# The inverse transform's last stage: one 96 by 96 block-diagonal matmul, or two of 48 by 48 in the row halves of the array

## The chip, the cores and the metric

The kernel runs on one core of a Trainium2 chip. The metric is the device time of one execution in microseconds, the median of several runs. Five engines work side by side, each through its own list of instructions in order: TensorE (PE in the profile; its weight loads are listed as PEld), VectorE (DVE), ScalarE (ACT), GpSimd (POOL), and SyncE (SP), which here only issues DMAs. Matmul results land in PSUM, eight banks of 512 fp32 words per partition.

## The reference

Eight sequences of 3072 rows of 256 numbers go through a Fourier layer, and the result through a feed-forward layer with a three-way maximum:

```python
X = np.fft.rfft(x, axis=1)
Yr = Xr @ w_r - Xi @ w_i + b_r
Yi = Xr @ w_i + Xi @ w_r + b_i
Yr = np.sign(Yr) * np.maximum(np.abs(Yr) - lam, 0.0)      # lam = 0.01, the same for Yi
y = np.fft.irfft(Yr + 1j * Yi, n=3072, axis=1)
h = np.maximum(np.maximum(y @ w1, y @ w2), y @ w3)        # 256 -> 768
out = h @ w_out                                           # 768 -> 256
```

## The kernel before

The length 3072 is split as 48 x 64, and each transform is done in two matmul stages with tables that the host makes. A batch is one of the eight sequences. It goes through: `stage_a` (48-point transform; two row halves of the array, at partitions 0 to 47 and 64 to 111, and two column halves, fp32), a round trip through DRAM (`a_d`), `stage_b` (64-point transform, px), `stage_w` (the complex weights, py, then bias and soft threshold), `stage_q` (64-point inverse, pz), another round trip through DRAM (`z_d`), and then, chunk by chunk, the last 48-point inverse stage, `inverse` (pi). There are 8 chunks in a batch, 64 in all, each of 384 output positions.

After `inverse` a chunk goes through the feed-forward layer in six slots, one for each 128 of the 768 hidden columns: `up` (12 matmuls of 384 columns into two pu banks, then the maximum and a split), and one slot later `down` (pd, 9 matmuls of 256 columns, and over the last slots 18 more for the third weight, which is folded with w_out).

Nearly every operand is held as two fp16 parts, high and low, and a product is three matmuls: high x high, high x low, low x high (`mm3`, lines 133 to 135). So lines 133 to 135 appear under many tiles in the profile. The split itself is `split_scaled` (lines 127 and 128): an ACT copy that rounds to fp16, then a DVE subtraction for the rest.

The order of work: the main loop (lines 853 to 878) writes `up`, `down` and then what a list of events holds for that slot, which are the stages of the next batch. The event list (lines 689 to 703) is written out by hand with positions in slots. Around the change, `load_z` of the next chunk is called in slot 1, `split_z` in slot 3, `inverse` in slot 4. Its result is used from slot 0 of the next chunk, one `up` and one `down` later. The framework's scheduler then lays down each engine's list, with its own estimates of cost; on ACT, for instance, the copy of the next z stands between the two copies of pi in many chunks.

The tiles that matter here:

- zq, one buffer: a quad of z, 96 partitions (p, m) by 4 x 256 fp32, where p is one of two groups of four n2 positions and m one of 48 coefficients. Two DMAs on SP's queue fill it (line 713).
- zh and zl, one buffer each: its two fp16 parts (lines 720 to 723).
- ga_sb, the table: for each of 32 quads a 96 by 96 matrix with two 48 by 48 blocks on the diagonal and zeros elsewhere, in two fp16 parts (lines 49 to 53, 154).
- pi, taken by `ff_tile` from the ring of four PSUM banks called "ff", which px, py, pz and pa use as well. `inverse` takes one bank for each half h of the 256 columns, does 12 matmuls into it, and splits it into yh and yl; then comes the other h.
- xq, the input rows: its rows 32 to 63 are set to zero on POOL before the DMA (line 413). These are POOL's main work.

Of the kernel before, what the change touches and what calls it, by code (L numbers as in the profile page):

```python
# [9 lines left out]
F32 = mybir.dt.float32  # L10
F16 = mybir.dt.float16
# [9 lines left out]
T_SCALE, Y_SCALE, H_SCALE, Q_SCALE = 2.0**-15, 2.0**-14, 2.0**-23, 2.0**12  # L21


def dft_tables():

    n, n1n, n2n = 3072, 48, 64
    n1, n2, tp = np.arange(n1n), np.arange(n2n), 2 * np.pi
    fa, ga = np.zeros((n1n, n1n)), np.zeros((n1n, n2n, n1n))
    for m in range(46):
        k1, c = 1 + m // 2, m % 2
        ph = tp * ((k1 * n1) % n1n) / n1n  # L40
        fa[:, m] = np.cos(ph) if c == 0 else -np.sin(ph)
        ph = tp * ((k1 * (n2n * n1[None, :] + n2[:, None])) % n) / n
        ga[m] = (2.0 / n) * (np.cos(ph) if c == 0 else -np.sin(ph))
    alt = (-1.0) ** n1
    fa[:, 46], ga[46] = 1.0, 1.0 / n
    fa[:, 47], ga[47] = alt, alt[None, :] / n
    fa2 = np.zeros((112, 64))
    fa2[0:48, 0:48] = fa2[64:112, 0:48] = fa
    g5 = ga.reshape(n1n, 8, 2, 4, n1n)
    ga2 = np.zeros((2, n1n, 8, 4, 2, n1n))  # L50
    for p in range(2):
        ga2[p, :, :, :, p] = g5[:, :, p]
    ga2 = ga2.reshape(96, 32, 96)
    sg = np.where(n2 >= 32, -1.0, 1.0)

    def forward(k1):
        ang = tp * ((n2[:, None] * (k1 + n1n * n2[None, :])) % n) / n
        co, si = np.cos(ang), np.sin(ang)
        b = np.zeros((2, n2n, 2, n2n))
        b[0, :, 0], b[1, :, 0] = co, si  # L60
        b[0, :, 1], b[1, :, 1] = -si * sg, co * sg
        return b.reshape(128, 128)

    ang = tp * ((n2[:, None] * n2[None, :]) % n2n) / n2n
    co, si = np.cos(ang), np.sin(ang)
    q = np.zeros((2, n2n, 2, n2n))
    q[0, :, 0], q[1, :, 0] = co, -si * sg[:, None]
    q[0, :, 1], q[1, :, 1] = si, co * sg[:, None]
    bs, qs = np.zeros((2, n2n, 2, n2n)), np.zeros((2, n2n, 2, n2n))
    alt = (-1.0) ** n2  # L70
    bs[0, :, 0, 0], bs[0, :, 1, 0] = 1.0, alt
    qs[0, 0, 0, :], qs[1, 0, 0, :] = 1.0, alt
    for f in range(1, n2n):
        c, k = (0, n1n * f) if f < 32 else (1, 24 + n1n * (f - 32))
        ph = tp * ((k * n2) % n) / n
        bs[c, :, 0, f], bs[c, :, 1, f] = np.cos(ph), -np.sin(ph)
        qs[0, f, c, :], qs[1, f, c, :] = 2 * np.cos(ph), -2 * np.sin(ph)
    q, bs, qs = (v.reshape(128, 128) for v in (q, bs, qs))
    mb = [forward(k1) for k1 in range(1, 24)] + [bs]
    mq = [q, qs]  # L80

    def halves(v, scale):
        v = v * 2.0**scale
        hi = v.astype(np.float16)
        return np.ascontiguousarray(np.stack([hi, (v - hi).astype(np.float16)], 1))

    return (
        fa2.astype(np.float32),
        halves(ga2, SG),
        halves(np.stack(mb, 1), SB),  # L90
        np.ascontiguousarray(np.stack(mq + mb, 1)).astype(np.float32),
        np.eye(128, dtype=np.float32),
    )
# [3 lines left out]
def fourier_maxout_kernel(  # L97
    ctx: ExitStack, tc: tile.TileContext, x, w_r, w_i, b_r, b_i, w1, w2, w3, w_out, fa, ga, mb, mq, ident, out
):
    nc = tc.nc  # L100
    NB, S, D = x.shape
    FF = w1.shape[1]
    P = 128
    N1, N2 = 48, 64
    XR = 112
    KD = D // P
    NF = FF // P
    NQ = 4
    NCH = N2 // 8
    NT = 8 * N1  # L110
# [3 lines left out]
    const = ctx.enter_context(tc.tile_pool(name="const", bufs=1))  # L114
    fft = ctx.enter_context(tc.tile_pool(name="fft", bufs=2))
# [9 lines left out]
    def split_scaled(hi, lo, src, scale):  # L125
        h = hi if hi.dtype == F16 else hi.bitcast(F32)
        nc.scalar.activation(out=hi, in_=src, func=AF.Copy, scale=scale)  # L127
        nc.vector.scalar_tensor_tensor(  # L128
            out=lo, in0=src, scalar=scale, in1=h, op0=ALU.mult, op1=ALU.subtract
        )  # L130

    def mm3(o, lh, ll, rh, rl, start=True, stop=True, **kw):
        nc.tensor.matmul(o, lh, rh, start=start, stop=False, **kw)  # L133
        nc.tensor.matmul(o, lh, rl, start=False, stop=False, **kw)  # L134
        nc.tensor.matmul(o, ll, rh, start=False, stop=stop, **kw)  # L135
# [4 lines left out]
    def ff_tile(name):  # L140
        tag = spare[0]
        if len(spare) > 1:
            spare.append(spare.pop(0))
        return ps.tile([P, 512], F32, name=name, tag=tag, bufs=4 if tag == "ff" else 2)
# [6 lines left out]
    mb_all = const.tile([P, 4 * NJP * P], F16, name="mb_all")  # L151
    mb_sb = mb_all.rearrange("p (i k m) -> p i k m", i=2, k=2 * NJP)
    mb_f = mb_all.bitcast(F32).rearrange("p (k m) -> p k m", k=2 * NJP)
    ga_sb = const.tile([96, 2, N2 // 2, 2 * N1], F16, name="ga_sb")
    wch = const.tile([P, KD, 4, D], F16, name="wch")
    wcl = const.tile([P, KD, 4, D], F16, name="wcl")
    wuh = const.tile([P, 2, KD, FF], F16, name="wuh")
# [12 lines left out]
    def quad_tile(name):  # L170
        return fft.tile([XR, NQ * D], F32, name=name, bufs=1 if name == "zq" else 2)
# [213 lines left out]
    st = {}  # L385
# [303 lines left out]
    for q in range(NCH + 2, NB * NCH):  # L689
        b, i = divmod(q, NCH)  # L690
        p = i if b == 1 else (b - 2) * SLOTS + NF * i + 2
# [3 lines left out]
    for b in range(1, NB):  # L695
        for k in range(-2, NJP + 1):
            p = 8 + 2.2 * (k + 2) if b == 1 else (b - 1) * SLOTS + 2.8 * (k + 2)
# [10 lines left out]
            fn(i)  # L708

    def load_z(b, c):  # L710
        zq = quad_tile("zq")[0:96]
        for p in range(2):
            nc.sync.dma_start(
                out=zq[p * N1:p * N1 + N1].rearrange("p (n d) -> p n d", n=NQ),
                in_=batch(b, "z")[:, 8 * c + 4 * p:8 * c + 4 * p + 4, :],
            )
        st["zq"] = zq

    def split_z(b):
        zh = fft.tile([96, NQ, D], F16, name="zh", bufs=1)  # L720
        zl = fft.tile([96, NQ, D], F16, name="zl", bufs=1)
        split_scaled(*(t.rearrange("p n d -> p (n d)") for t in (zh, zl)), st["zq"], st[b, "su"][0][0:96])
        st["z"] = zh, zl

    def inverse(b, c):
        zh, zl = st["z"]
        yh, yl = (ffn.tile([P, KD, NT], F16, name=n, bufs=2) for n in ("yh", "yl"))
        for h in range(KD):
            py = ff_tile("pi")
            pv = py[:, 0:NT].rearrange("q (p i m) -> q i p m", p=2, i=NQ)  # L730
            for n2 in range(NQ):
                mm3(
                    pv[:, n2], *(t[:, n2, h * P:(h + 1) * P] for t in (zh, zl)),
                    *(ga_sb[:, i, c * NQ + n2, :].rearrange("q (p m) -> q p m", p=2) for i in range(2)),
                )
            split_scaled(
                *(t[:, h].rearrange("p (m n) -> p m n", n=8) for t in (yh, yl)),
                py[:, 0:NT].rearrange("p (n m) -> p m n", n=8), Y_SCALE,
            )
        return yh, yl  # L740

# [102 lines left out]
    for q in (NCH, NCH + 1):  # L844
        split_x(q)
        stage_a(q)
    load_z(0, 0)
    split_z(0)
    y = inverse(0, 0)
    del spare[1:]  # L850
    spare[0] = "ff"
# [61 lines left out]
```

## Time and profile before

| what | value |
|---|---|
| time, median of 3 runs | 1835.04 us (1834.65 to 1837.48) |
| profiled execution | 1835.95 us, span 1833.8 us, granted TensorE clock 0.987 |
| matmuls into pi (three lines of 512) | 1536, median 207 ns recorded each |
| splits of pi | 128 ACT copies of 490 ns, 128 DVE subtractions of 551 ns |
| splits of z | 64 ACT copies of 1148 ns, 64 DVE subtractions of 1276 ns |
| zero-fills on POOL (xq) | 56 of 942 ns |

A recorded matmul includes the time that its last columns take to pass through, which overlaps with the next matmul; so the sum of durations says less than the distance between starts. Matmul groups are named by the tile that they write: pi is the stage that is changed.

### The profile page before, as it was taken

The page shows a single profiled execution, that of the slowest core. Times are in us where ns is not written, and L with a number is a line of the kernel's source. Part 1 is how long each engine was busy: PE and PEld are TensorE (multiplying, and loading weights), DVE is VectorE, ACT ScalarE, POOL GpSimd, SP SyncE. Part 2 cuts the span into 40 slices and gives each one's busy share as a digit, 9 for nine tenths or more (in the row PEclk, how much of TensorE's full clock was granted, in tenths as well). Part 3 has the DMA queues.
Part 4 walks back from the last instruction along what each step waited for, and adds up shares of the span by engine and source line. Part 5 has one row for each costly group of instructions (what it writes and reads, how often), then busy time and mean ns, then how long its engine had stood idle before and what let it go on. Part 6 is the DMA issues. An engine that isn't in the chain of part 4 may idle for free.

```text
span 1833.8 us, 36240 instructions
## 1 busy us (share of the span) xinstructions
PE 1779.5 (97%) x14535; PEld 1288.8 (70%) x14535; DVE 1296.9 (71%) x2580; ACT 964.0 (53%) x1930; POOL 71.7 (4%) x119
## 2 busy tenths in 40 slices
PE   4979999999999999999999999999999999999999
PEld 2756677777677777777677776777767677777776
DVE  1897788668886688758886688866888568864443
ACT  2335565455554566455554555645655455544443
POOL 0001000000000000100000000000000000000000
PEclk6999999999999999999999999999999999999999
DMA  8734432233323323233322422223322321212110
GB/s 246 230 114 109 127 105 87 67 113 98 93 62 101 96 84 93 67 113 81 87 81 70 121 87 87 76 78 105 96 87 67 96 57 60 63 37 58 35 35 27
DMA packets 116570, 164.99 MB, mean 90 GB/s; under 512 B 13137, under 2 KB 88914, under 8 KB 116306
## 3 DMA queue, kind: packets, MB, share of 16 engines
q1 hardware_dynamic: 54450, 87.15, 17.1%
q10 hardware_dynamic: 61952, 75.52, 13.4%
q8 instruction: 114, 1.87, 0.4%
q14 instruction: 54, 0.44, 0.1%
HBM read 87.13 MB, written 75.50 MB: 89 GB/s over the span
## 4 chain that ended last, share of the span: by engine, by line
PE 71%; DVE 7%; DMA 2%; issue 2%; ACT 1%; ACTq 1%; SPq 0%; POOL 0%; DVEq 0%; POOLq 0%
PE pu L133 11%; PE pu L135 11%; PE pu L134 11%; PE pd L135 7%; PE pd L134 7%; PE pd L133 7%; PE py L133 2%; PE py L134 2%; PE py L135 2%; PE pa L438 2%; DMA xq<-in_x_dram 2%; DVE u L621 1%; DVE hh L128 1%; PE pi L135 1%; PE pi L133 1%
## 5 line engine op out<-in xcount | busy, mean ns | idle before, releaser
L133 PE MATMUL pu<-yh,wuh 128*128 128x384 f16 x1536 | 502.6, 327 | 2.0 <-DVE h L755 1.9
L134 PE MATMUL pu<-yl,wuh 128*128 128x384 f16 x1536 | 502.1, 327 | 1.7 <-DVE yl L128 1.5
L135 PE MATMUL pu<-yh,wul 128*128 128x384 f16 x1536 | 502.2, 327 | 0.0
L127 ACT ACTIVATE hh<-h 128x384 f16<-128x384 f32 x384 | 200.4, 522 | 355.6 <-DVE h L755 350.2
L755 DVE TENSOR_TENSOR h<-pu,c 128x384 f32<-128x384 f32 x384 | 212.6, 554 | 174.5 <-PE pu L135 112.9
L135 PE MATMUL pd<-woh,hh 128*128 128x256 f16 x1152 | 314.1, 273 | 6.4 <-DVE hh L128 6.3
L134 PE MATMUL pd<-wol,hh 128*128 128x256 f16 x1152 | 314.1, 273 | 0.0
L133 PE MATMUL pd<-woh,hh 128*128 128x256 f16 x1152 | 314.1, 273 | 0.0
L128 DVE SCALAR_TENSOR_TENSOR hh<-h,hh 128x384 f16<-128x384 f32 x384 | 213.3, 555 | 107.8 <-ACT hh L127 106.4
L753 ACT ACTIVATE c<-pu 128x384 f32<-128x384 f32 x384 | 186.6, 486 | 135.7 <-PE pu L135 125.6
L133 PEld LDWEIGHTS <-wuh 128*128 128x128 f16 x1536 | 150.2, 98 | 112.9 <-issue 32.8
L135 PEld LDWEIGHTS <-wul 128*128 128x128 f16 x1536 | 150.1, 98 | 102.8 <-issue 3.8
L134 PEld LDWEIGHTS <-wuh 128*128 128x128 f16 x1536 | 150.4, 98 | 84.1 <-issue 4.4
L621 DVE SCALAR_TENSOR_TENSOR u<-py,s1x,cs 64x256 f32<-64x256 f32 x308 | 148.6, 482 | 47.7 <-ACT cs L632 34.0
L133 PE MATMUL py<-wch,tt 128*128 128x256 f16 x504 | 137.5, 273 | 0.0
L134 PE MATMUL py<-wcl,tt 128*128 128x256 f16 x504 | 137.5, 273 | 0.0
L135 PE MATMUL py<-wch,tt 128*128 128x256 f16 x504 | 137.5, 273 | 0.0
L133 PEld LDWEIGHTS <-hh 128*128 128x128 f16 x1152 | 112.5, 98 | 31.6 <-issue 1.6
L134 PEld LDWEIGHTS <-hh 128*128 128x128 f16 x1152 | 112.6, 98 | 30.1
L135 PEld LDWEIGHTS <-hh 128*128 128x128 f16 x1152 | 112.5, 98 | 25.4 <-DVE hh L128 11.0
L782 ACT ACTIVATE o<-pd,s1u 128x256 f32<-128x256 f32 x192 | 83.3, 467 | 66.7 <-PE pu L135 22.2
L424 DVE TENSOR_REDUCE mxx<-xq 112x1 f32<-112x512 f32 x112 | 74.4, 679 | 43.1 <-DMA xq<-in_x_dram 39.8
(185 smaller groups left out, 3065.1 us busy)
## 6 DMA issues: line engine op xcount, KB each, us to landing
aj<-a_d SPq DMA_DIRECT2D x96, 256.0 KB, 2.8
z_d<-zs ACTq DMA_DIRECT2D x96, 256.0 KB, 2.2
zq<-z_d SPq DMA_DIRECT2D x128, 192.0 KB, 3.2
out_dram<-o ACTq DMA_DIRECT2D x192, 128.0 KB, 2.3
a_d<-aq ACTq DMA_DIRECT2D x124, 192.0 KB, 3.3
xq<-in_x_dram SPq DMA_DIRECT2D x120, 192.0 KB, 3.7
rw<-in_moe_w_dram SPq DMA_DIRECT2D x12, 384.0 KB, 6.8
xr<-in_x_dram SPq DMA_DIRECT2D x16, 96.0 KB, 3.8
```

The costliest lines, as they stand in the source:

```text
L127: nc.scalar.activation(out=hi, in_=src, func=AF.Copy, scale=scale)
L128: nc.vector.scalar_tensor_tensor(out=lo, in0=src, scalar=scale, in1=h, op0=ALU.mult, op1=ALU.subtract)
L133: nc.tensor.matmul(o, lh, rh, start=start, stop=False, **kw)
L134: nc.tensor.matmul(o, lh, rl, start=False, stop=False, **kw)
L135: nc.tensor.matmul(o, ll, rh, start=False, stop=stop, **kw)
L424: nc.vector.tensor_reduce(out=batch(b, "x")[0:XR, 2 * q4 + i:2 * q4 + i + 1], in_=xp, axis=AX.X, op=ALU.max, apply_absolute_value=True,)
L438: nc.tensor.matmul(pa[r][64 * c:64 * c + 64], fr[rows], xs[c][rows], start=True, stop=True)
L621: nc.vector.scalar_tensor_tensor(out=u[64 * c:64 * c + 64, j], in0=pk[r], scalar=inv[r], in1=c1[r], op0=ALU.mult, op1=ALU.add,)
L753: nc.scalar.activation(out=c1, in_=pu[0], func=AF.Relu)
L755: nc.vector.tensor_tensor(out=h32, in0=pu[1], in1=c1, op=ALU.max)
L782: nc.scalar.activation(out=o, in_=pd[t], func=AF.Copy, scale=st[b, "su"][1])
```

## The change

The table is kept as its two 48 by 48 blocks, one on partitions 0 to 47 and one on 64 to 111. z is laid out the same way, in a tile of 112 partitions of its own (zp), whose rows 32 to 63 are set to zero on POOL at each load, ahead of the DMA that fills rows 0 to 47. Each block-diagonal matmul becomes two, one for each block, on row half 0 and row half 1 of the array, and each half writes its own PSUM bank, in which now both h lie. The two splits follow after all 48 matmuls, one for each bank, and each writes every second run of four positions of yh and yl.

```diff
-    ga2 = np.zeros((2, n1n, 8, 4, 2, n1n))
+    ga2 = np.zeros((112, 8, 4, n1n))
     for p in range(2):
-        ga2[p, :, :, :, p] = g5[:, :, p]
-    ga2 = ga2.reshape(96, 32, 96)
+        ga2[64 * p:64 * p + n1n] = g5[:, :, p]
+    ga2 = ga2.reshape(112, 32, n1n)
...
-    ga_sb = const.tile([96, 2, N2 // 2, 2 * N1], F16, name="ga_sb")
+    ga_sb = const.tile([XR, 2, N2 // 2, N1], F16, name="ga_sb")
...
     def load_z(b, c):
-        zq = quad_tile("zq")[0:96]
+        zq = fft.tile([XR, NQ * D], F32, name="zp", bufs=1)
+        nc.gpsimd.memset(zq[32:64], 0.0)
         for p in range(2):
             nc.sync.dma_start(
-                out=zq[p * N1:p * N1 + N1].rearrange("p (n d) -> p n d", n=NQ),
+                out=zq[64 * p:64 * p + N1].rearrange("p (n d) -> p n d", n=NQ),
...
     def split_z(b):
-        zh = fft.tile([96, NQ, D], F16, name="zh", bufs=1)
-        zl = fft.tile([96, NQ, D], F16, name="zl", bufs=1)
+        zh = fft.tile([XR, NQ, D], F16, name="zh", bufs=1)
+        zl = fft.tile([XR, NQ, D], F16, name="zl", bufs=1)
...
     def inverse(b, c):
         zh, zl = st["z"]
         yh, yl = (ffn.tile([P, KD, NT], F16, name=n, bufs=2) for n in ("yh", "yl"))
+        pi = [ff_tile("pi") for _ in range(2)]
         for h in range(KD):
-            py = ff_tile("pi")
-            pv = py[:, 0:NT].rearrange("q (p i m) -> q i p m", p=2, i=NQ)
             for n2 in range(NQ):
-                mm3(
-                    pv[:, n2], *(t[:, n2, h * P:(h + 1) * P] for t in (zh, zl)),
-                    *(ga_sb[:, i, c * NQ + n2, :].rearrange("q (p m) -> q p m", p=2) for i in range(2)),
-                )
+                o = (n2 * KD + h) * N1
+                for lz, lg in ((zh, 0), (zh, 1), (zl, 0)):
+                    for p in range(2):
+                        r = slice(64 * p, 64 * p + N1)
+                        nc.tensor.matmul(
+                            pi[p][:, o:o + N1], lz[r, n2, h * P:(h + 1) * P], ga_sb[r, lg, c * NQ + n2, :],
+                            start=lz is zh and lg == 0, stop=lz is zl,
+                        )
+        for p in range(2):
             split_scaled(
-                *(t[:, h].rearrange("p (m n) -> p m n", n=8) for t in (yh, yl)),
-                py[:, 0:NT].rearrange("p (n m) -> p m n", n=8), Y_SCALE,
+                *(t.rearrange("p h (m n) -> p (h m) n", n=8)[:, :, 4 * p:4 * p + 4] for t in (yh, yl)),
+                pi[p][:, 0:NT].rearrange("p (n q) -> p q n", n=NQ), Y_SCALE,
             )
         return yh, yl
```

More of the change, by code (lines that the diff above doesn't have):

```diff
@@ L719, in split_z @@
     def split_z(b):
-        zh = fft.tile([96, NQ, D], F16, name="zh", bufs=1)
-        zl = fft.tile([96, NQ, D], F16, name="zl", bufs=1)
-        split_scaled(*(t.rearrange("p n d -> p (n d)") for t in (zh, zl)), st["zq"], st[b, "su"][0][0:96])
+        zh = fft.tile([XR, NQ, D], F16, name="zh", bufs=1)
+        zl = fft.tile([XR, NQ, D], F16, name="zl", bufs=1)
+        split_scaled(*(t.rearrange("p n d -> p (n d)") for t in (zh, zl)), st["zq"], st[b, "su"][0][0:XR])
         st["z"] = zh, zl
```

## The prediction

> **What bounds the kernel now.** I read the engines' shares first, then the two stretches before and after 170 us, then TensorE's own waits. The columns of the second view are stretch, length, and busy us (count) of PE, PEld, DVE, ACT and POOL.
>
> ```profile
> span 1833.8 us, 36240 instructions
> PE 1779.5 (97%) x14535; PEld 1288.8 (70%) x14535; DVE 1296.9 (71%) x2580; ACT 964.0 (53%) x1930; POOL 71.7 (4%) x119
> ```
> ```profile
> 0.00:170.00 170.00, 130.31 (x675) 92.25 (x676) 115.72 (x289) 63.35 (x125) 7.23 (x14) 0.86 0.59 176
> 170.00:1833.80 1663.80, 1649.18 (x13863) 1196.58 (x13860) 1181.15 (x2291) 900.68 (x1806) 64.51 (x105) 1.00 0.28 81
> ```
> ```profile
> PE pd L135 <- DVE hh L128: 6.3, 10, 0.9
> ...
> PE pu L133 <- DVE h L755: 1.9, 6, 0.4
> PE pi L135 <- DVE zl L128: 1.5, 1, 1.5
> PE pu L134 <- DVE yl L128: 1.5, 4, 0.4
> ```
>
> From 170 us on TensorE has 1649.18 of 1663.80 us filled, at full clock (1.00); 14.6 us are idle. The waits named there for DVE, 6.3 + 1.9 + 1.5 us, are most of it. So TensorE sets the end, and what one `inverse` takes of its queue is worth its price nearly 64 times. DVE at 71% and ACT at 53% bind only in short bursts.
>
> A matmul's recorded duration is not what it costs, because matmuls are pipelined; the distance from start to start is. Here is one `inverse` on TensorE between its neighbours (start, duration, engine, line):
>
> ```profile
> 937.68 0.27 PE L135 MATMUL py<-wch,tt 128*128 128x256 f16 x1
> 937.79 0.21 PE L133 MATMUL pi<-ga_sb,zh 96*128 96x96 f16 x1
> 937.84 0.20 PE L134 MATMUL pi<-ga_sb,zh 96*128 96x96 f16 x1
> ...
> 938.77 0.21 PE L135 MATMUL pi<-ga_sb,zl 96*128 96x96 f16 x1
> 938.81 0.33 PE L133 MATMUL pu<-yh,wuh 128*128 128x384 f16 x1
> ```
>
> From 937.79 to 938.81 are 24 matmuls in 1.02 us: 42.5 ns for each of 96 columns. There is no gap at either side (py to pi 0.11 us, what a 256-column matmul always takes). All 24 weight loads hide behind the streaming.
>
> **The change, part by part.** 24 matmuls of 96 rows by 96 columns become 48 of 48 rows by 48 columns, alternating between rows 0 to 47 and 64 to 111. The before kernel has a stage that already uses the array in parts, `stage_a` (pa, L438: row halves into separate PSUM tiles, and column halves as well). It is the nearest row for all that is new here:
>
> ```profile
> 900.62 0.22 PE L134 MATMUL px<-mb_all,ah 128*128 128x128 f16 x1
> 900.68 0.22 PE L135 MATMUL px<-mb_all,al 128*128 128x128 f16 x1
> 900.83 0.66 PE L438 MATMUL pa<-xq,fr 48*64 48x512 f32 x4
> ```
> ```profile
> 900.83 1.09 PE L438 MATMUL pa<-xq,fr 48*64 48x512 f32 x8
> 901.85 0.34 PE L133 MATMUL pu<-yh,wuh 128*128 128x384 f16 x1
> 902.02 0.33 PE L134 MATMUL pu<-yl,wuh 128*128 128x384 f16 x1
> ```
> ```profile
> L438 PE MATMUL pa<-xq,fr x8: 588/614/641, 900.8 to 901.3; 48*64 48x512 f32 x8
> ```
>
> *Entering.* px matmuls follow each other at 56 ns, but from the last px to the first pa it is 0.15 us: 0.094 us are lost when the array goes from whole to parts. *Leaving.* A matmul outlasts its streaming by 0.22 - 0.056 = 0.164 us. The eight pa end at 900.83 + 1.09 = 901.92, so their streaming ends at 901.756, and the next full matmul starts at 901.85: 0.094 us again. Today's `inverse` runs in whole-array form and pays neither; the new one pays both. I take the pa price, though pa's parts are quarters and in fp32.
>
> *First weight load.* After each of the two gaps the first load isn't hidden. Where a load itself waited, the rows show its size:
>
> ```profile
> 916.79 0.10 PEld L135 LDWEIGHTS <-hh 128*128 128x128 f16 x1 [1.18 <-DVE hh L128]
> 916.80 0.10 PEld L133 LDWEIGHTS <-hh 128*128 128x128 f16 x1
> ```
> ```profile
> 916.79 0.28 PE L135 MATMUL pd<-woh,hh 128*128 128x256 f16 x1 [0.91 <-DVE hh L128]
> 916.91 0.27 PE L133 MATMUL pd<-woh,hh 128*128 128x256 f16 x1
> 917.02 0.27 PE L134 MATMUL pd<-wol,hh 128*128 128x256 f16 x1
> ```
>
> The second load starts 0.01 us after the first, and the matmul behind takes 0.12 instead of 0.11 us: a 128-column f16 load holds the array for 10 to 15 ns. So 0.01 us at each switch, and in the stream a load hides behind a 48-column matmul.
>
> *The 48 matmuls.* 42.5 ns at 96 columns and 56 at 128 give 0.42 ns a column and 2.2 ns fixed, thus 22.4 ns at 48 columns. For a pair (one matmul per half) the trace has no row, so I bound it. Low: the halves run side by side, 22.4 ns. High: they take turns, 44.8 ns. pa speaks for the low end: four matmuls of up to 0.641 us fit into 0.66 us, so they start within 0.02 us, 6.5 ns apart, and run at once, in both row halves. I take side by side with the fixed part paid twice: 48 x 0.42 + 2 x 2.2 = 24.6 ns. 24 pairs make 0.59 us.
>
> *Sum for one inverse:* 0.094 + 0.01 + 0.59 + 0.094 + 0.01 = 0.80 us against 1.02: 0.22 us less. The first inverse waits for its data; 63 x 0.22 = 13.9 us.
>
> *What is given back.* Where TensorE next waits for DVE, it arrives earlier and waits longer. The hh waits are 10, the largest group; 10 x 0.22 = 2.2 us at most, nothing at least. I take 1.4, so 12.5 us net.
>
> *Evacuation.* Two ACT copies and two DVE subtractions of 384 columns remain (0.48 and 0.55 us in the rows below), in runs of 4 instead of 8; I see no row in which run length costs time, and take the same durations. What moves is their start: today the first copy starts when half the matmuls are done, then it must wait for all, and the first `up` of the next chunk needs both halves at once. One chunk whose inverse ends at 968.09:
>
> ```profile
> 967.85 0.48 ACT L127 ACTIVATE yh<-pi 128x384 f16<-128x384 f32 x1
> ...
> 968.41 0.49 ACT L127 ACTIVATE yh<-pi 128x384 f16<-128x384 f32 x1
> ```
> ```profile
> 970.83 0.55 DVE L128 SCALAR_TENSOR_TENSOR yl<-pi,yh 128x384 f16<-128x384 f32 x1
> ```
> ```profile
> 972.34 0.33 PE L133 MATMUL pu<-yh,wuh 128*128 128x384 f16 x1
> 972.51 0.33 PE L134 MATMUL pu<-yl,wuh 128*128 128x384 f16 x1
> ```
>
> The last yl ends at 971.38, and TensorE needs it at 972.51: 1.1 us of cover. The first copy moves by some 0.4 us. The cover is one whole `up` and `down` between inverse and use. Where it is gone already (yl waits: 4 times, 1.5 us), needing both parts at once costs up to three pu matmuls, 0.49 us each time, 2 us in all; the waits for h and hh that follow there absorb part of it. I count it into the 1.4.
>
> *The z tile.* 64 more memsets on POOL and a wait of z's first DMA for each. A memset of this size, and the z transfer's round:
>
> ```profile
> L413 POOL MEMSET xq<- x56: 942/942/954, 13.6 to 1396.5; 32x1024 f32 x56
> ```
> ```profile
> 914.99 1.28 DVE L128 SCALAR_TENSOR_TENSOR zl<-zq,s0u,zh 96x1024 f16<-96x1024 f32 x1
> ```
> ```profile
> 916.33 0.79 SPq L713 DMA_DIRECT2D zq<-z_d  x2
> ```
> ```profile
> 938.97 1.15 ACT L127 ACTIVATE zh<-zq,s0u 96x1024 f16<-96x1024 f32 x1
> ```
> ```profile
> zq<-z_d SPq DMA_DIRECT2D x128, 192.0 KB, 3.2
> ```
>
> zl frees the tile at 916.27; memset 0.94, then the DMA's 3.2: ready near 921, needed at 938.97, so 18 us of cover. On SP's queue the aj and x loads behind z come 1 us later; on POOL's queue the next xq memset can stand behind zl. x loads are ordered several slots ahead, so I price both at nothing; without cover each would cost 1 us a chunk. Splitting 112 rows instead of 96 costs nothing in time. The ga table halves; it is loaded in the first stretch, where other transfers are awaited. Nothing.
>
> **The sum:** the profiled execution took 1835.95 us, 2.15 beyond its span, and stands 0.9 above the median of the three runs. 1835.95 - 12.5 = 1823.5, and on the median's footing 1822.5; I say 1823.
>
> **Rivals.**
>
> *The halves take turns* (slower). If TensorE doesn't overlap the two halves of f16 matmuls this short, 48 x 22.4 = 1.075, with 0.208 for the switches 1.283 us: 0.263 us more, x 63 = 16.6 us: 1851.6. It decides from a pair pitch of 33.8 ns upward, where 24 pairs and switches reach 1.02. Against it stand the 6.5 ns between pa's starts; for it, that pa streams 512 columns and these 48. Here belongs a rule of the Trainium skill, TensorEngine Tiling, section Instruction Overhead: a matmul costs about 60 cycles however few its columns, and one should not tile a dimension that is already small. By an estimate from it (25 ns at the 2.4 GHz that the skill's page TensorE: Matmul & The Clock Gate gives in Part 1, not overlapped) the inverse would take 1.41 us, and the kernel 1859; if the floor holds for each half by itself, the sum stays as forecast. pa's starts speak for the second.
>
> *The loads take turns,* while the matmuls overlap: a pair then takes two loads, 30 ns. 0.72 + 0.208 = 0.93 us, 0.09 less: 5.8 us, 1829. pa's four loads also start 6.5 ns apart, which speaks against it.
>
> *The loads of halves become slow.* pa's fp32 loads of 64 columns cost 641 - 588 = 53 ns; 128 columns at that rate 106 ns a pair: 2.54 + 0.21, 1.73 us more each time, 1944. Today's 96-row loads are fast, so incomplete rows alone don't make them slow.
>
> *The waits take it back.* The planner orders ACT, DVE and POOL anew. If the burst waits above (9.7 us) double, 13.9 - 9.7 - 2 is about 2 us: 1833, no change.
>
> **How the numbers follow.** This kernel's measurement can't tell 0.2%, 3.7 us, from nothing. The forecast (1817 to 1829, pair pitch 22 to 28 ns): 0.58. Loads in turn (near 1829): 0.10. Waits take it back: 0.10. Halves in turn: 0.18. Slow loads: 0.04. Faster 0.68, same 0.10, slower 0.22. The range goes from the low bound (0.75 us an inverse, 17.2 us: 1818, with 2 for fewer waits) to the halves in turn: 1816 to 1852; the likeliest case's own range is 1817 to 1829.
>
> **What would show it.** The pi group with 48x48 rows lasting 0.80 us up to the first pu; 0.15 to 0.2 us between the matmul ahead and the first pi; pairs 6 to 10 ns apart within and about 25 ns from pair to pair. Start distances of an even 22 ns say turns. PE's waits for yl, h and hh should stay near 10 us. If the pi group is short and the time isn't, the waits took it. A wait of zh for POOL or for z's DMA would prove the z part mispriced.

## The result: 0.6% slower, though the matmuls cost what was forecast

| | before | after |
|---|---|---|
| median of the runs of one call | 1836.26 us | 1846.86 us |
| ratio, 95% interval | | 1.0059, 1.0039 to 1.0079 |
| profiled execution, span | 1835.95, 1833.8 us | 1847.45, 1845.7 us |
| TensorE's late starts (below) | 14.9 us | 42.4 us |

The forecast was 1823 us. Here are the head of the page, the stretch after 170 us, and TensorE's waits of the changed kernel, in the columns explained above.

```profile
span 1845.7 us, 39502 instructions
PE 1774.3 (96%) x16071; PEld 1263.1 (68%) x16071; DVE 1303.3 (71%) x2580; ACT 961.7 (52%) x1930; POOL 128.2 (7%) x183
```
```profile
170.00:1845.70 1675.70, 1643.38 (x15346) 1172.05 (x15338) 1187.11 (x2291) 897.60 (x1804) 117.88 (x166) 1.00 0.28 81
```
```profile
PE pu L134 <- DVE yl L128: 14.2, 10, 2.2
PE pd L135 <- DVE hh L128: 9.3, 21, 1.1
...
PE pu L133 <- ACT c L758: 2.9, 8, 0.7
```

TensorE is busy for less time, but idle for 32.3 us after 170 us instead of 14.6. The wait for yl went from 1.5 to 14.2 us, that for hh from 6.3 to 9.3. One inverse of the changed kernel on TensorE (start, duration, engine, line; rows with the same operands are drawn together):

```profile
692.24 0.27 PE L135 MATMUL py<-wch,tt 128*128 128x256 f16 x1
692.44 0.22 PE L736 MATMUL pi<-ga_sb,zh 48*128 48x48 f16 x4
692.50 0.18 PE L736 MATMUL pi<-ga_sb,zl 48*128 48x48 f16 x2
692.53 0.21 PE L736 MATMUL pi<-ga_sb,zh 48*128 48x48 f16 x4
...
693.03 0.18 PE L736 MATMUL pi<-ga_sb,zl 48*128 48x48 f16 x2
693.15 0.34 PE L133 MATMUL pu<-yh,wuh 128*128 128x384 f16 x1
```

The first three pairs take 0.09 us (692.44 to 692.53); behind the first pair it is 39 ns, from then on 25 ns a pair, and the two matmuls of a pair start 0 to 4 ns apart. From py to pi it is 0.20 us instead of 0.11, from the first pi to the first pu 0.71: with the 0.096 us lost on entering, 0.80 us in place of 1.02. So 0.21 us are saved per inverse, and in the undisturbed last chunks (the 57th to the 63rd) each step from inverse to inverse is 0.21 us shorter than before.

What is set against it is late starts. Busy time hides part of these, since a pipelined matmul still counts as busy after its successor could have started. So I also took every trace from the first pi of the second chunk to that of the 63rd (61 inverses) and added up, over all f16 matmuls outside pi whose successor is neither in pi nor in pa, by how much the next start came later than these columns take undisturbed (0.162 us for 384, 0.109 for 256, 0.216 for 512, 0.056 for 128), where it was more than 12 ns. These are the *late starts*. They are of the one execution that was profiled, and executions of one kernel lie up to 11 us apart (e5 below: 1828.87 to 1839.81 us, and the profiled one is the slowest), so a difference of 1 or 2 us says little. Before 14.9, after 42.4: 27.5 more, against 61 x 0.21 = 12.8 saved, so a loss of 14.7; the stretch itself grew by 13.5 us (1616.2 to 1629.7).

**Where it waits.** The longest late start of a batch comes in its fifth chunk, in five of the eight batches. These five chunks hold 21.4 of the 42.4 us and 10.7 of the 27.5 that were added; another 10.2 were added in the first two chunks of batches. Here is a fifth one (the chunk numbered 20 from 0). VectorE before:

```profile
692.69 0.69 DVE L424 TENSOR_REDUCE mxx<-xq 112x1 f32<-112x512 f32 x1 [2.10 <-DMA xq<-in_x_dram]
693.29 0.55 DVE L128 SCALAR_TENSOR_TENSOR hh<-h,hh 128x384 f16<-128x384 f32 x1
693.75 1.99 DVE L621 SCALAR_TENSOR_TENSOR u<-py,s1x,cs 64x256 f32<-64x256 f32 x4
695.77 0.56 DVE L128 SCALAR_TENSOR_TENSOR yl<-pi,yh 128x384 f16<-128x384 f32 x1
...
699.91 0.55 DVE L128 SCALAR_TENSOR_TENSOR hh<-h,hh 128x384 f16<-128x384 f32 x1
```

and after, with the TensorE row that waits for it:

```profile
694.76 0.69 DVE L424 TENSOR_REDUCE mxx<-xq 112x1 f32<-112x512 f32 x1 [2.52 <-DMA xq<-in_x_dram]
695.36 0.55 DVE L128 SCALAR_TENSOR_TENSOR hh<-h,hh 128x384 f16<-128x384 f32 x1
695.83 1.99 DVE L621 SCALAR_TENSOR_TENSOR u<-py,s1x,cs 64x256 f32<-64x256 f32 x4
697.85 0.69 DVE L424 TENSOR_REDUCE mxx<-xq 112x1 f32<-112x512 f32 x1
698.45 0.68 DVE L644 TENSOR_TENSOR u<-u,bias 128x512 f32<-128x512 f32 x1
699.16 0.56 DVE L128 SCALAR_TENSOR_TENSOR yl<-pi,yh 128x384 f16<-128x384 f32 x1
699.64 0.42 DVE L578 TENSOR_SCALAR t<-u 128x512 f32<-128x512 f32 x1
699.97 0.55 DVE L128 SCALAR_TENSOR_TENSOR yl<-pi,yh 128x384 f16<-128x384 f32 x1
```
```profile
700.57 0.32 PE L134 MATMUL pu<-yl,wuh 128*128 128x384 f16 x1 [2.21 <-DVE yl L128]
```

In both, VectorE stands over 2 us before the x input's maximum (mxx, L424), because x has not landed; everything behind it in its list, hh and the yl of this chunk, is late by that. After the change it is worse: the inverse ends 0.9 us later than before (693.15 against some 692.3) but x lands 2.07 us later, and a second mxx and the bias now stand ahead of both yl. The two lists differ. On ScalarE the copy of z also moved ahead of both copies of y (after: zh 693.28, yh 694.34; before: yh 691.97, zh 692.44, yh 693.50). It stands ahead of both in 44 of 63 chunks; before, it stood ahead of both in none, between them in 21 and behind both in 42.

### The profile page after: what moved, and what is told of

Its sections match the earlier page's. It is cut to its first block, busy times and chain, and to the rows that moved or that the text cites. A ratio compares the mean times of both kernels' runs of the same rounds, so it can differ in the third digit from the quotient of the medians.

```text
span 1845.7 us, 39502 instructions
## 1 busy us (share of the span) xinstructions
PE 1774.3 (96%) x16071; PEld 1263.1 (68%) x16071; DVE 1303.3 (71%) x2580; ACT 961.7 (52%) x1930; POOL 128.2 (7%) x183
## 4 chain that ended last, share of the span: by engine, by line
PE 67%; DVE 15%; DMA 7%; issue 7%; ACT 2%; POOL 1%; ACTq 1%; SPq 1%; DVEq 0%; POOLq 0%
PE pu L133 10%; PE pu L134 10%; PE pu L135 9%; PE pd L135 7%; PE pd L133 6%; PE pd L134 6%; DMA xq<-in_x_dram 3%; PE pa L438 3%; PE py L133 2%; PE py L135 2%; PE py L134 2%; DVE u L621 2%; PE pi L736 2%; DVE h L760 2%; DVE hh L128 1%
## 5 line engine op out<-in xcount | busy, mean ns | idle before, releaser
L134 PE MATMUL pu<-yl,wuh 128*128 128x384 f16 x1536 | 501.2, 326 | 14.5 <-DVE yl L128 14.2
L712 POOL MEMSET zp<- 32x1024 f32 x64 | 60.4, 944 | 723.7 <-DVE zl L128 666.7
```

What stands on the lines that cost most here:

```text
L712: nc.gpsimd.memset(zq[32:64], 0.0)
```

## The experiments

Each time is the median against the kernel before in the same call, which lay between 1834.4 and 1836.6 us. No run is numbered e7.

| run | time, us | ratio (95% interval) | late starts, us |
|---|---|---|---|
| e1 after, y ahead of z | 1831.61 | 0.9976 (0.9967 to 0.9985) | 27.3 |
| e2 before, own z tile | 1835.08 | 1.0003 (0.9993 to 1.0012) | 15.3 |
| e3 before, late banks | 1835.65 | 1.0004 (0.9994 to 1.0013) | 17.9 |
| e4 after, z tile zeroed once | 1846.92 | 1.0070 (1.0053 to 1.0087) | 38.8 |
| e5 e1 and e4 together | 1833.02 | 0.9993 (0.9982 to 1.0004) | 33.0 |
| e6 e5 with two z tiles | 1832.44 | 0.9989 (0.9980 to 0.9997) | 27.0 |
| e8 after, z behind hh, two z tiles | 1823.23 | 0.9942 (0.9930 to 0.9953) | 17.5 |
| e9 before, y ahead of z | 1834.14 | 0.9993 (0.9985 to 1.0002) | 14.8 |
| e10 before, z behind hh | 1821.04 | 0.9920 (0.9906 to 0.9935) | 3.5 |
| e11 after, z behind hh | 1818.50 | 0.9908 (0.9891 to 0.9924) | 13.3 |
| e12 e10 with late banks | 1819.71 | 0.9911 (0.9898 to 0.9925) | 2.4 |
| e13 e10 with own z tile | 1820.00 | 0.9916 (0.9902 to 0.9930) | 3.6 |
| e14 e10 with 19 matmuls of 24 | 1808.35 | 0.9846 (0.9833 to 0.9860) | 4.6 |
| e15 e11, nine pairs more | 1837.53 | 1.0007 (0.9997 to 1.0018) | 18.6 |
| e16 e10, columns split | 1836.16 | 1.0004 (0.9995 to 1.0014) | 8.0 |
| e17 e16 with a bank per half | 1835.32 | 1.0004 (0.9993 to 1.0015) | 7.8 |
| e18 e11 in e13's order | 1815.65 | 0.9890 (0.9876 to 0.9903) | 8.6 |
| e19 after in before's order | 1832.88 | 0.9985 (0.9976 to 0.9994) | 25.0 |

### e1 to e3: order, z tile, late banks, each alone

e1 makes the split of z issue behind both splits of y; the order edge costs no wait:

```diff
-            split_scaled(*(t.rearrange("p h ...
+            st["ylast"] = split_scaled(*(t.rearrange("p h ...
...
+        with ExitStack() as after_y:
+            for ins in st.pop("ylast", ()):
+                after_y.enter_context(tc.issue_after(ins.ins))
             split_scaled(..., st["zq"], st[b, "su"][0][0:XR])
```

> The changed kernel, with the copy and the subtraction of the next z laid behind those of pi (an ordering edge on ACT and one on DVE). Theory 'order': in the changed kernel both banks of pi are complete only after the last matmul, while zh's buffer is free two matmuls earlier, so the scheduler puts the 1.15 us copy of z ahead of both copies of pi, y comes some 1 to 1.5 us late, and TensorE waits for it. With the order put right the 0.21 us an inverse stay: 1821 to 1828 us, TensorE's waits for yl under 3 us. Theory 'late banks': y is late because both banks end at once, whatever the order: 1841 or more. Theory 'z tile': POOL and SP queues delay the loads: 1841 or more.

15 us came back, though not all that this theory gave (1821 to 1828 us); late starts 42.4 to 27.3, and the wait for yl fell from 14.2 to 4.9 us:

```profile
PE pu L135 <- DVE yl L128: 4.9, 5, 1.1
```

The order of ScalarE's and VectorE's work is most of the loss.

e2 is the kernel before with a z tile of its own and the memset:

```diff
-        zq = quad_tile("zq")[0:96]
+        zq = fft.tile([XR, NQ * D], F32, name="zp", bufs=1)
+        nc.gpsimd.memset(zq[0:32], 0.0)
+        zq = zq[0:96]
```

> The kernel before, with z in a tile of its own that POOL partly zeroes at each load (32 rows, so that one of the two DMAs has to wait for it, as in the change); the matmuls and splits stay whole. Theories 'order' and 'late banks': 1833 to 1840 us, as before. Theory 'z tile': 10 us or more over the kernel before, 1845 or more.

No difference. e3 is the kernel before with the two blocks of h alternating, so that both banks come complete at the end:

```diff
-        for h in range(KD):
-            py = ff_tile("pi")
-            for n2 in range(NQ):
+        pi = [ff_tile("pi") for _ in range(KD)]
+        for n2 in range(NQ):
+            for h in range(KD):
                 mm3(...)
+        for h in range(KD):
             split_scaled(...)
```

> The kernel before, with the two column halves h interleaved, so that both pi banks are complete only at the end of the 24 whole-array matmuls; in this kernel's ACT list the copies of pi stay ahead of the copy of z. Theory 'order': 1831 to 1840 us, no clear change. Theory 'late banks': TensorE waits for y as in the change, with no gain to set against it: 1848 to 1862 us. Theory 'z tile': as before, 1833 to 1840.

No difference either. Neither part does harm alone.

### e4 to e6: is the rest z's tile?

e4 zeroes a constant z tile once instead of at each load; e5 adds e1's edges; e6 has two such tiles in turn.

```diff
-        zq = fft.tile([XR, NQ * D], F32, name="zp", bufs=1)
-        nc.gpsimd.memset(zq[32:64], 0.0)
+        i = (b * NCH + c) % 2                     # e6; e4 and e5 have one tile
+        if ("zp", i) not in st:
+            st["zp", i] = const.tile([XR, NQ * D], F32, name=f"zp{i}")
+            nc.gpsimd.memset(st["zp", i][32:64], 0.0)
+        zq = st["zp", i]
```

> The changed kernel, with one fixed z tile whose rows 32 to 63 are zeroed once at the start instead of at each of 64 loads. Theories 'order' and 'late banks': 1842 to 1850 us, like the changed kernel. Theory 'z tile': 1830 or less.

> The changed kernel with the order put right (as in e1_y_first) and z in one fixed tile zeroed once. e1 came to 1831.6 us, some 8 us over what TensorE's saving alone gives. Theory 'z reload': in the first chunk of each batch z's reload starts only when the subtraction of z ends, the memset adds 1 us to it, ACT stands at the copy of z, and behind it the copy c that frees a pu bank; without the memset 1825 to 1829 us. Rival 'both parts at once': the rest is that the first up needs both splits, in the DVE bursts; then as e1, 1830 to 1833.

> As e5_y_first_zero_once, but with two fixed z tiles, so that a reload no longer waits for the subtraction of the z before. Theory 'z reload': 1820 to 1826 us, and ACT's waits for z's DMA go from 18 to under 8 us. Rival 'both parts at once': 1829 to 1833, although ACT's waits for the DMA go.

e4 is as slow as the change, e5 and e6 as e1. The theory that z's reload takes the rest fell.

### e8 to e11: where z stands

e8 lays the split of z behind the split of hh of its own chunk (its expectation says slot 2; the place is slot 3), with e6's two tiles. e11 does it with the changed kernel's one tile, e10 in the kernel before. e9 puts e1's edges into the kernel before.

```diff
-        split_scaled(hh[:, 0], hh[:, 1], h32, H_SCALE)
+        st["hlast"] = split_scaled(hh[:, 0], hh[:, 1], h32, H_SCALE)
...
+        with ExitStack() as after_h:
+            for ins in st.get("hlast", ()):
+                after_h.enter_context(tc.issue_after(ins.ins))
             split_scaled(..., st["zq"], ...)
```

> The changed kernel with two fixed z tiles, and the split of z laid behind the last split of the hidden layer in slot 2 of its own chunk, so far from the inverse. If the place of z's copy and subtraction among the others (1.15 and 1.28 us) is what delays y and h: 1817 to 1825 us. If moving them only shifts the delay to the hidden layer's splits, whose slot they then share: 1830 or more.

> The kernel before with the same ordering edges as in e1_y_first: z's split behind those of pi. If the halves are worth what TensorE saves (0.21 us an inverse, 13 us) at equal order, this takes 1837 to 1846 us, e1's time and 6 to 14 more. If the ordering edges alone make the kernel faster, 1832 or less, and e1's gain isn't the halves'.

> The kernel before, whole-array matmuls and all, with z's split laid behind the split of the hidden layer in slot 3 of its own chunk (as in e8_z_in_slot, whose text says slot 2 and means the same place). If z's place costs the kernel before as well, it gains by this too, and e8's 11 us under the kernel before are not the halves' alone: 1826 to 1831 us. If the kernel before has nothing to gain, 1833 to 1837, and the halves are worth their 11 to 13 us at equal order.

> The changed kernel as it is, one z tile with its memset at each load, and only the ordering edges of e8_z_in_slot added. z's load then starts only after the split in slot 3 and has a whole chunk but for the inverse. If the second z tile and the dropped memsets matter: 1826 to 1832 us. If the place of z's split is all: 1821 to 1825, as e8.

e9 fell between its two theories: y ahead of z gains nothing in the kernel before. e10 and e11 came out faster than any theory said. With z behind hh the kernel before gains 15 us too, with no change to a matmul: it also had waits that its order made. Other work moved with z (some 140 of ScalarE's 1930 instructions and some 215 of VectorE's 2580 stand in another order), so the gain is that of the new order, not of z's copy alone. VectorE's wait for x, before (first row) and in e10 (second fence), and TensorE's waits in e10:

```profile
DVE mxx L424 <- DMA xq<-in_x_dram: 39.8, 21, 2.6
```
```profile
DVE mxx L425 <- DMA xq<-in_x_dram: 18.1, 10, 2.9
```
```profile
PE pd L136 <- DVE hh L128: 0.8, 3, 0.4
PE pu L134 <- DVE h L759: 0.7, 2, 0.3
```

x arrives in time more often, and the once-a-batch wait for hh is gone. But the halves gain only 2.5 us at either order (e1 against e9, e11 against e10), of 13.

### e12 and e13: late banks and z tile at the good order

The edits of e3 and e2, on e10.

> The kernel before (whole 96 by 96 blocks) with z's copy and subtraction laid behind the last subtraction of hh of its own chunk, as in the run that took 1821.04 us, and now with the two blocks of `h` alternating inside each of the four groups, so that both PSUM banks of pi are complete only at the end, as they are in the changed kernel. The halves' matmuls save 13 us when counted alone, but with z in this place the halves took 1818.5 us against 1821.04: 10 us are missing. Theory A, both banks coming complete together takes them back (the first copy of y starts later, two copies and two subtractions come as one burst): 1826 to 1832 us, TensorE's waits after 170 us above 8 us where the whole array had 2. Theory B, something else of the change (its own z tile, the columns of y that a copy writes) takes them back: 1819 to 1823 us. Theory C, the saving itself does it, since TensorE 0.2 us ahead in every chunk meets the other engines' chains sooner: 1819 to 1823 us too, and the run beside it tells C from B.

> The kernel before with z's copy and subtraction in the same place, and z's transfer going into a buffer of its own of 112 rows, of which 32 are set to zero on POOL before each transfer, as the changed kernel does it, instead of into the ring of four buffers that it shares. TensorE's matmuls are those of before. Theory B, that buffer takes back the 10 us that are missing between the halves' saving of 13 us and their gain of 2.5 us at equal order (one buffer means that the next transfer waits for the last subtraction of z): 1826 to 1832 us, with waits of TensorE for zh, zl or c. Theory A (both banks complete together) and theory C (TensorE ahead meets the other engines' chains): 1819 to 1823 us.

Both at e10's time. A and B as worded fell; C was left, that a saving here is worth little. (z never had a ring of four buffers, as the second text has it: it has one buffer in both kernels.)

### e14 and e15: is a saving worth anything?

```diff
+                if h * NQ + n2 < 3:                       # e14
                     mm3(pv[:, n2], *lhs, *g)
+                else:                                     # without zl
+                    nc.tensor.matmul(pv[:, n2], lhs[0], g[0], start=True, stop=False)
+                    nc.tensor.matmul(pv[:, n2], lhs[0], g[1], start=False, stop=True)
```
```diff
-                for lz, lg in ((zh, 0), (zh, 1), (zl, 0)):
+                terms = [(zh, 0), (zh, 1)] + [(zl, 0)] * (10 if h == KD - 1 and n2 == NQ - 1 else 1)  # e15
```

> The kernel before with z's copy and subtraction behind hh of their own chunk (1821.04 us), whole 96 by 96 blocks, and five of the eight matmuls with zl left out of each inverse, so that 19 are left of 24: the output lacks those products. At 42 ns each TensorE saves 0.21 us per inverse, 13 us in all, as much as the halves do, with nothing else of the halves in it. Theory C, TensorE 0.2 us earlier in each chunk meets the chains of the other engines, so most of the saving is waited away: 1815 to 1820 us, with some 8 to 12 us of waits for hh, h, c or o after 170 us where there were 2. Theory D, something that only the halves have (two 48-row matmuls at a time, 48 more instructions, both banks written side by side) costs the missing 10 us: 1807 to 1810 us, waits as in the 1821 us kernel.

> The changed kernel with z's copy and subtraction behind hh of their own chunk (1818.5 us), and the last pair of zl matmuls of each inverse issued ten times instead of once: nine more pairs at 24 to 25 ns make the group 0.22 us longer, as long as the whole array's with its entering and leaving, and the output has that product ten times. Theory C, the 0.2 us per chunk are waited away anyway: 1818 to 1822 us, with TensorE's waits after 170 us back near 2 us. Theory D, the halves cost some 10 us on their own: 1830 to 1833 us, with the waits for hh, h and c still there.

e14 sinks theory C too: 0.21 us less per inverse in the whole array gave 12.7 us of 13. e15 lies above both theories: the padding cost 19, its 14 and 5 more of late starts. Its lists aren't e11's (some 45 places on ScalarE and 90 on VectorE differ), so these 5 may be the order's. The stretch after 170 us of e14 and of e11:

```profile
170.00:1800.00 1630.00, 1627.24 (x13526) 1181.58 (x13524) 1184.44 (x2290) 895.68 (x1800) 60.13 (x105) 1.00 0.28 83
```
```profile
170.00:1800.00 1630.00, 1622.32 (x15265) 1164.59 (x15262) 1184.06 (x2282) 894.23 (x1796) 119.41 (x166) 1.00 0.29 83
```

2.8 us idle against 7.7. The halves bring waits that the same saving in the whole array does not, each in the order that the scheduler made for it.

### e16 and e17: 48 matmuls without row halves

```diff
-                mm3(pv[:, n2], ...)
+                for p in range(2):                        # e16; e17: p inside, into pi[p]
+                    for lz, lg in ((zh, 0), (zh, 1), (zl, 0)):
+                        nc.tensor.matmul(
+                            pv[:, n2, p], lz[:, n2, h * P:(h + 1) * P],
+                            ga_sb[:, lg, c * NQ + n2, p * N1:p * N1 + N1], ...
```

> The kernel before with z's copy and subtraction behind hh of their own chunk (1821.04 us), each 96-row 96-column matmul of pi issued as two 96-row 48-column ones: 48 matmuls per inverse as in the changed kernel, no row halves, the banks and copies those of before (one per `h`). At 21 to 25 ns a matmul TensorE's own time grows by 0 to 0.18 us per inverse, 0 to 11 us in all, so the waits are to be read, not the time alone. Theory F, the doubled number of matmuls changes the order that the scheduler gives to ScalarE's and VectorE's work, and that order costs the missing 10 us: TensorE idle 8 to 13 us after 170 us, 1829 to 1842 us. Theory G, row halves themselves, or a bank per half with its copies: idle 1 to 3 us after 170 us, 1820 to 1832 us.

> As the run before, with 48 matmuls of 96 rows and 48 columns per inverse, and now a PSUM bank per half and the copies of the changed kernel (each for 4 of 8 columns of both `h`): all that the halves are but the row halves. Built, ScalarE and VectorE do their work in exactly the order of the changed kernel with z behind hh (1818.5 us). Theory F, that order (or the copies of both `h` at once) costs the missing 10 us: TensorE idle 8 to 14 us after 170 us, 1829 to 1844 us. Theory G, the row halves themselves cost it: idle 1 to 3 us after 170 us, 1820 to 1832 us. If this run waits and the one beside it doesn't, the bank per half and its copies are the cause; if both wait, the number of matmuls and the order that it gives.

Here the group took 1.22 us up to the next pu, 25.4 ns for each matmul, so 12 us of the time are TensorE's own. TensorE is idle for 5.6 and 5.0 us from 170 to 1780 us (e10 1.8): below what F gave, above G. Late starts are 8.0 and 7.8 us, 4.5 and 4.3 over e10's. That both wait alike says that the bank per half and its copies add nothing here; the count of matmuls, and the order that the scheduler makes of it, adds some 4 us. e17's lists are e11's, place by place, and e11 has 13.3: in the same order the row halves, or the time that they save, add 5.5.

### e18 and e19: the halves in the whole array's order

All of ScalarE's and VectorE's instructions are chained in a given order (a packed list of 2345 places, DMA issues among them, and of 2580), with order edges alone:

```diff
+def keep_order(tc, engine, packed):
...
+    for x, y in zip(order, order[1:]):
+        tc.add_manual_dep(traced[y], traced[x].name, info, reason="order")
...
     down(*prev)
+    keep_order(tc, mybir.EngineType.Activation, ACT_LIST)
+    keep_order(tc, mybir.EngineType.DVE, DVE_LIST)
```

> The changed kernel with z behind hh (1818.5 us), and all 2345 instructions of ScalarE's list and 2580 of VectorE's held in the order that they have in the whole array with z behind hh and z's own buffer (1820.0 us), edge by edge; some 115 and 104 of them move. TensorE's matmuls are the halves, its order is the same but for the first chunks. Theory F, the order that the scheduler gave to ScalarE and VectorE when it counted 48 matmuls costs the missing 10 us: 1820.0 - 13 = 1807, so 1805 to 1811 us, late starts of TensorE's matmuls between the second and the last inverse about 3 to 5 us as in the run of 1820.0 us. Theory G, the halves cost it by themselves (row halves, or copies over both `h` that come complete together): 1815 to 1820 us, late starts still about 13 us.

> The changed kernel as it is, with no edge for z or y, but all of ScalarE's and VectorE's instructions held in the order that the kernel before has (some 277 and 251 move). It does exactly what the prediction added up: the matmuls of the halves, z's own buffer and the late banks, with every other engine's work where it was. Theory F, the order that the scheduler made anew is what turned the saving into a loss: 1835 - 13 = 1822, so 1820 to 1826 us, late starts of TensorE 13 to 17 us as in the kernel before. Theory G, something of the halves costs beside the order: 1829 to 1838 us. If it comes near 1847 us, order was not the cause at all.

e19 settles the loss. With nothing but the order put back, the change goes from 1846.86 to 1832.88 us, and late starts from 42.4 to 25.0: the scheduler's new order cost 14 us. It also sinks the theory that order is all: 1822 was due, and late starts stayed 10.1 above the kernel before's, as theory G has it. The same chunk as above in e19, VectorE and then TensorE's two waits:

```profile
692.69 0.69 DVE L467 TENSOR_REDUCE mxx<-xq 112x1 f32<-112x512 f32 x1 [2.21 <-DMA xq<-in_x_dram]
...
695.78 0.56 DVE L171 SCALAR_TENSOR_TENSOR yl<-pi,yh 128x384 f16<-128x384 f32 x1
...
696.85 0.55 DVE L171 SCALAR_TENSOR_TENSOR yl<-pi,yh 128x384 f16<-128x384 f32 x1
...
699.91 0.55 DVE L171 SCALAR_TENSOR_TENSOR hh<-h,hh 128x384 f16<-128x384 f32 x1
```
```profile
697.46 0.32 PE L177 MATMUL pu<-yl,wuh 128*128 128x384 f16 x1 [1.11 <-DVE yl L171]
700.52 0.28 PE L178 MATMUL pd<-woh,hh 128*128 128x256 f16 x1 [0.90 <-DVE hh L171]
```

and TensorE before:

```profile
698.25 0.32 PE L133 MATMUL pu<-yh,wuh 128*128 128x384 f16 x1 [0.32 <-DVE h L755]
700.51 0.28 PE L135 MATMUL pd<-woh,hh 128*128 128x256 f16 x1 [0.90 <-DVE hh L128]
```

VectorE does the same work at the same times to 0.01 us, as x lands at the same time, and TensorE leaves this chunk at 700.5 in both. It came to this chunk only 0.2 us ahead, though. To chunk 12 it came 1.52 us ahead, and there x's maximum started earlier as well, before and in e19:

```profile
476.21 0.69 DVE L424 TENSOR_REDUCE mxx<-xq 112x1 f32<-112x512 f32 x1 [2.33 <-DMA xq<-in_x_dram]
```
```profile
475.03 0.69 DVE L467 TENSOR_REDUCE mxx<-xq 112x1 f32<-112x512 f32 x1 [2.58 <-DMA xq<-in_x_dram]
```

Behind these waits TensorE was still 1.17 us ahead. So x's chain moves with TensorE for the most part, and the wait for it takes only a part of the lead.

Compared chunk by chunk with the kernel before, e19 is 0.21 us shorter in each undisturbed chunk and loses at a few places: 1.67 us longer in chunk 12; 2.3 longer in chunk 32, to which it came 0.9 ahead; 0.9 in 22 and 40, 0.55 in 16 and 44. From chunk 17 to 53 it is mostly behind the kernel before, by up to 1.7 us, so it lost more than a lead there. In sum it is ahead by 1.7 us after 61 inverses, of 12.8. By place, the 10.1 us are:

- some 1.7 in the fifth chunks, at the waits behind x's maximum;
- some 4.2 in the first two chunks of batches, where ScalarE stands for transfers of z or aj (in chunk 32 for aj 2.86 us, 0.54 before);
- some 4.1 behind four long DMA issues on ScalarE's queue (chunks 12, 22, 40 and 44).

The one in chunk 12, before and then in e19, with what waits behind it:

```profile
486.89 1.20 ACTq L783 DMA_DIRECT2D out_dram<-o  x2
```
```profile
485.72 2.55 ACTq L831 DMA_DIRECT2D out_dram<-o  x2
488.32 0.60 ACT L170 ACTIVATE tt<-px 128x512 f16<-128x512 f32 x1 [2.27 <-issue]
```
```profile
495.29 0.32 PE L176 MATMUL pu<-yh,wuh 128*128 128x384 f16 x1 [0.71 <-DVE h L803]
```

The second of the two issues took 1.91 us, where 0.55 is usual; ScalarE stood, and through tt, VectorE and h the delay reached TensorE 7 us later. The last section says what these long issues have in common.

e18 is the fastest kernel here that computes everything, 1815.65 us. It gained 4.4 over e13, whose order it has, so some 8 of the 12.8 are missing. Its late starts are 8.6 (in an execution 2 us below its median): 4.7 below e11's, which the order must have made, the lists being all that was changed, and 5.0 above e13's. That lies between theories F and G, and its time at G's lower end. Some 2.6 of these 5.0 follow long issues too (chunks 12, 22, 34 and 44).

**Open** is where the rest of these 5 us comes from: e14 kept its saving, but in an order that the scheduler made for its own 19 matmuls, and a saving of the whole array in a fixed order was not tried. So it isn't known whether any saving under a kept order loses this much, or only that of the halves.

## Why the prediction was wrong

*Entering, leaving, the 48 matmuls, sum for one inverse:* right. Entering 0.096 us (forecast 0.094), leaving: pi to pu 0.112 us, of which 25 ns are streaming (0.09; forecast 0.094), pairs at 25 ns (24.6), together 0.80 us as forecast, 0.21 us less than before. The *first weight load* can't be told apart in these figures. Inside a pair the starts are 0 to 4 ns apart, not 6 to 10. Halves or loads in turn, and slow loads, are out. The fixed part was misjudged without harm: 22.4 ns were given to a 48-column matmul by itself, and e16 shows 25.4. The Trainium skill states an issue floor near 25 ns for 1 to 64 columns (TensorE: Matmul & The Clock Gate, Back-to-back issue gap), and e16 agrees; its floor holds for each row half by itself, since a pair took the same 25 ns, so the rule on small dimensions that was weighed as a rival did not decide.

*What is given back* is one step that failed. It took 1.4 us, from "10 x 0.22 = 2.2 us at most". With the order of ScalarE's and VectorE's lists unchanged, e19 measured 10.1 us of added late starts; by the medians only 2.7 of the 12.8 us were gained (1835.55 to 1832.88). The bound looked only at the waits for hh that were there. At these, in the fifth chunks, e19 gave back some 1.7 us, which is inside the bound. The other 8.3 came where the kernel before hardly waited: in the first chunks of batches and behind long DMA issues. The bound also charged each wait with the saving of one chunk, while TensorE carries its lead on: to chunk 12 it came 1.52 us ahead, and to chunk 13 it came 0.15 behind.

*Evacuation* holds the other step that failed, and the larger one: the order. The prediction held all other work in its place, and left "the planner orders ACT, DVE and POOL anew" to a rival with a chance of 0.10 that priced a doubling of the burst waits at 9.7 us and ended at 1833. The order is that rival's mechanism, but its cost was 17.4 us of late starts (42.4 to 25.0), enough to turn the sign. The cover of 1.1 us for yl was that of an undisturbed chunk; in the fifth chunk of a batch there was none, and the wait there reached 2.2 us. That z's copy slid ahead of y's is most of it: e1 holds only this pair and lets the scheduler lay the rest, and its late starts, 27.3, come near the 25.0 of the whole old order.

*The z tile* was priced at nothing, and the runs bear that out (e2, e4, e13). The sign that was named against it did come, since ScalarE's wait of zh for z's DMA grew from 8.7 to 15.4 us (170 to 1780 us); but e6 took it to 6.0 and was no faster than e1. And the 18 us of cover were not general: in the first chunk of a batch zl ends only 0.77 us ahead of the inverse that reads it (0.69 before).

*What would show it:* "If the pi group is short and the time isn't, the waits took it" is what came. The waits for yl, h and hh, which should have stayed near 10 us, became 24.4 in TensorE's waits (14.2 + 9.3 + 0.9).

## What to carry over

Where TensorE is 99% busy but waits at a few regular places, a saving ahead of them isn't worth its sum: here 10.1 of 12.8 us went again with all other work in its old order. Before pricing the saving, read for each such place which chain ends the wait, and whether it starts earlier when TensorE does. Don't bound what is given back by the waits that are there now, nor by one chunk's share: a lead runs on to the next wait, and chains with little slack, here ScalarE's, become new waits. Where a scheduler lays down the lists, a change of one stage's instructions can reorder everything else: hold the order fixed to learn what the change itself is worth, and try the order alone, which here gave 15 us with no change to a matmul and six times what the halves gave.

## What the runs showed of the hardware

*Half clock after a short pause.* The changed kernel has five late starts of 2.37 us (2.2 of it idle), one in the fifth chunk of each of five batches. After two of them (chunks 20 and 36) TensorE ran at half clock for some 3.4 us. Stretch by stretch around the first:

```profile
698.40:701.90 3.50, 1.23 (x7) 0.67 (x7) 3.47 (x8) 0.74 (x2) 0.00 (x0) 1.00 0.00 0
701.90:705.40 3.50, 3.50 (x17) 2.15 (x15) 3.07 (x5) 2.00 (x5) 0.79 (x1) 0.51 0.22 75
705.40:708.90 3.50, 3.50 (x34) 2.63 (x33) 1.34 (x3) 2.69 (x7) 0.15 (x1) 1.00 0.78 222
```

The granted clock is 0.51 in the second, in which 17 matmuls ran against 34 in the third, and pd matmuls came 0.213 us apart in place of 0.109. So such a pause cost some 1.7 us beside its own length, by an estimate from 3.5 us at 0.51. It came once more each in e4 and e5, behind late starts of 2.37 and 2.26 us, and not in e1, whose longest is 2.0. Nothing in the kernel before stood long enough to show it; there the longest late start after the beginning is 1.07 us. The Trainium skill puts the fall to half clock after one idle window of about 3.4 us (TensorE: Matmul & The Clock Gate, Part 1). The length of the slow stretch agrees; the pause that brought it about was shorter than such a window, and the measurement decides. The Trainium skill also says there that the window runs freely, which would fit that only two of five pauses did it; no run here tests that.

*Long DMA issues beside instruction packets.* The four long issues of e19 start within 0.2 us of a 16 KB packet on the queue that the page calls q8 instruction. Its packets, before and in e19 (count, MB, share):

```profile
q8 instruction: 114, 1.87, 0.4%
```
```profile
q8 instruction: 126, 2.06, 0.5%
```

The count follows the number of TensorE's matmuls (111 in e14, 135 in e15), so these are TensorE's own instructions. Over the 20 traces, from 170 to 1780 us, 99 DMA issues on ScalarE's queue took over 0.9 us; at 88 of them an instruction packet of 8 or 16 KB began between 1.2 us ahead of the issue's start and 0.6 us behind it. Of the 7297 shorter issues 12% had one. So a change in the number of matmuls also moves the places where such a packet meets an issue. That the packet lengthens the issue is inferred from their meeting; no run moved one without the other.
